# A windowed-attention and geglu block on one Trainium2 core: a third copy buffer, a band in bf16, weights loaded slice by slice, and a sixth group of down corrections by seven products

## The chip, the core and the metric

The kernel runs on one core of one Trainium2 chip. TensorE (PE) multiplies matrices, VectorE (DVE), ScalarE (ACT) and GpSimd (POOL) work on what it leaves, and SyncE (SP) and ScalarE issue the transfers. Each engine takes its instructions in one fixed order and waits by semaphores for the others. The metric is the device time in microseconds (us) of one execution.

## The reference, cut to what matters

S = 2048 tokens, D = 640, H = 32 heads of 20, a window of 256 keys, F = 1536.

```python
def _A_ref(x, wqkv, wo):                     # x is layer-normed
    q, k, v = split((x @ wqkv))              # 32 heads of 20
    scores = einsum("bhqd,bhkd->bhqk", q, k) * 20 ** -0.5
    mask = (i - j >= 0) & (i - j < 256)
    p = softmax(where(mask, scores, -1e9))
    return einsum("bhqk,bhkd->bhqd", p, v) @ wo
h  = x + _A_ref(_layernorm(x), wqkv, wo)
h2 = h + (gelu(_layernorm(h) @ w_gate) * (_layernorm(h) @ w_up)) @ w_down
```

## The kernel before, in words

Everything is float32, and the big products are made on TensorE from 16-bit parts: a matrix is scaled by a power of two and split into a high half and a low half, and a product is three products of halves (high x high, high x low, low x high). For a part of the feed-forward matrices a scheme with sums replaces the plain one and saves a product in eight ("seven products").

**Stages.** (1) Load and split the three attention weights and the first tokens; (2) for chunks of 256 tokens, make queries and keys (the matmuls `mm<-xh,w0h` and the like for queries, `mm<-xh,w1h` for keys), copy them as two halves (`qks`), send them to DRAM (`qk`) and stack them into `qT` and `kT`; (3) for every block of 128 tokens compute scores by way of the wide banks `ra` and `rb`, first for the maxima (DVE's custom operation `junk<-ra` and `junk<-rb`, which also adds a mask or the `band`), then for the exponentials `pt` (ACT), mask them (POOL), multiply by the values (`pv<-pt,v`) and by the output weight; (4) the feed-forward, in 12 groups: 4 chunks of 512 tokens by 3 parts of F, each of 4 tiles of gate and up (`tp`, `ra`, `rb`) and then the down product (`mm`, `pv`).

**Who sets the order.** Every instruction goes through one helper, so the profile gives all of them line 199, and groups are told apart by tile names. A planner in `block_kernel` keeps a clock of estimated times for each engine while it writes the program. Each strand of work (a "lane": `load_lane`, `scale_lane`, `split_lane`, `qk_out`, `token_sums`, `dense_lane` and so on) says what its next step needs, and the loop at the end issues the first lane whose step could start about now. So a change of one buffer or one wait moves instructions on every engine. Until the first block has been scored, the loop issues a filler product where nothing else could run on TensorE:

```python
        else:
            if not pos["score"] and nc.t["tensor"] <= now:
                nc.tensor.matmul(pv[:, 0, :], ident16, ident16, start=True, stop=True)
```

In the trace they are `pv<-ident`; 235 of them run.

**Copies of queries and keys.** `qk_out` (L761): ACT writes the high half of one or two 128-column tiles into a `qks` buffer, DVE subtracts and writes the low half, ACT issues the transfer. There are two buffers, so the third copy waits until the first has been sent, and the `mm` bank that it reads stays full that long.

**Band.** `max_out` (L916) reads `band`, a 128x320 constant, beside the scores in PSUM, 448 times.

**Weights of the feed-forward.** The first gate, up and output weights come by slices (`wsl`). The other seven, `rest` in `load_lane` (L1641), are the down weight of part 0 and then gate, up and down of parts 1 and 2. Each is loaded whole into one staging tile `wst`, after the one before it is wholly split (`rest[i - 1].ready`). `scale` takes the largest absolute value of each slice, `split` writes the high half (ACT), and `low` the low half (DVE or POOL). A down weight is [128, 4, 640]: four slices of 640.

**Seven products.** `ORDER` lists the 12 groups, (0,0), (1,0), (0,1), (0,2), (1,1), (1,2) and then chunk 2 and chunk 3. For the groups in `SEVEN = ORDER[FIRST7:-1]`, with `FIRST7 = 6` five of them, the down product is `down7` (L1461): 88 matmuls of 320 columns, where `down` takes 96. It wants, for each such group, sums of the down weight (`seven_weights`: `ts`, two instructions of POOL and two of DVE, 1280 columns each) and of the tokens' factors (`seven_tokens`: `w9l`, four of POOL and four of DVE, 512 columns each). Eight results a group go by way of ACT into `w8l` and are added by DVE (`ht<-ht,w8l`, eight of 320 columns), and two come from the bank `pv`. `ah` and `al` are the halves of gelu(gate) times up, `gel` and `rs` its steps; `w10`, `w11`, `w12` are the halves of the down weights of parts 0, 1 and 2; `h0h`, `h0l`, `h1h`, `h1l` the normed tokens; `ws` the sums of gate and up weights.

Of the kernel before, what the change touches and what calls it, by code (L numbers as in the profile page):

```python
# [11 lines left out]
F32 = mybir.dt.float32  # L12
# [241 lines left out]
def block_kernel(ctx: ExitStack, tc: tile.TileContext, x, wqkv, wo, wg, wu, wd, out):  # L254
# [69 lines left out]
    def on(eng, *reads, when=None, after=None):  # L324
        f = need(*reads, when=when, eng=eng)
        if after is not None:
            return (eng,), lambda: max(f(), nc.others(after, eng))
        return (eng,), f
# [14 lines left out]
    nc.vector.tensor_copy(ident16, ident)  # L343
    mhalf = const.tile([P, 1], F32, name="mhalf")
    nc.vector.memset(mhalf, -0.5)
    ones = const.tile([P, P], F32, name="ones")
    nc.vector.memset(ones, 1.0)


    NS = 16  # L350
# [3 lines left out]
    class Weight:  # L354
# [5 lines left out]

        def __init__(self, src, shape, col, e=WE):
            self.src, self.shape, self.col, self.e = src, shape, col, e
            self.have = set()
            self.raw = {}

        @property
        def ready(self):
            return len(self.have) == self.shape[0]

        def load(self, room):  # L370
            for i in range(self.shape[0]):
# [16 lines left out]
            pos["used"] += self.sliced  # L388

        def scale(self, lane, tp="tp"):  # L390
            n = self.shape[0]
            am = nc.tile(lnp, [P, 8], F32, "am" + lane, 2 if lane == "0" else 1)
            nc.vector.memset(am[:, n:n + 1], _pow2(-100))
            for i in range(n):
                if self.hl and self.col != C_K:

                    yield on("scalar", self.raw[0, i])
                    nc.scalar.activation(self.hl[0][:, i, :], self.raw[0, i], AF.Abs,
                                         accum_out=am[:, i:i + 1])
                    continue  # L400
                yield on("vector", when=lambda: (0, i) in self.raw)
                yield on("vector", self.raw[0, i])
                nc.vector.tensor_reduce(am[:, i:i + 1], self.raw[0, i], axis=AX.X, op=ALU.max,
                                        apply_absolute_value=True)
                self.done_with()
            yield on("vector", am)
            nc.vector.tensor_reduce(am[:, 7:8], am[:, 0:n + 1], axis=AX.X, op=ALU.max)

            yield on("vector", am)
            nc.vector.tensor_scalar(am[:, 7:8], am[:, 7:8], _pow2(-self.e), None, op0=ALU.mult)  # L410
            hold = SETTLE if ffpools[1] else 0.0
            bound = need(am, slots=[tp])
            yield ("tensor",), lambda: bound() + hold
            t = bank(tp)
            nc.tensor.matmul(t[:, 0:P], am[:, 7:8].to_broadcast([P, P]), ident, start=True,
                             stop=True)
            pc = pw[:, self.col:self.col + 1]
            sc = sw[:, self.col:self.col + 1]
            yield soon("vector", t)
            nc.vector.tensor_reduce(am[:, 6:7], t[:, 0:P], axis=AX.X, op=ALU.max)  # L420
            done(tp)
            yield on("vector", am)
            nc.vector.tensor_scalar(pc.bitcast(I32), am[:, 6:7].bitcast(I32), 0x7F800000, None,
                                    op0=ALU.bitwise_and)
            yield on("vector", pc)
            nc.vector.tensor_scalar(sc.bitcast(I32), pc.bitcast(I32), -1, 0x7F000000,
                                    op0=ALU.mult, op1=ALU.add)
            self.scaled = True
            yield on("vector", pc)
            nc.vector.tensor_scalar(pc, pc, _pow2(self.e), None, op0=ALU.mult)  # L430
            self.known = True
# [6 lines left out]
        def split(self, pool, spread=0):  # L438
            self.room(pool)
            self.begun = True  # L440
            sc = sw[:, self.col:self.col + 1]
            for i in range(self.shape[0]):
                yield on("scalar", when=lambda: (1, i) in self.raw)
                yield on("scalar", sc, self.raw[1, i])
                nc.scalar.activation(self.hl[0][:, i, :], self.raw[1, i], AF.Copy, scale=sc)
                tasks.append(self.low(i, sc, i < spread))

        def low(self, i, sc, spread):
            hi, lo = (t[:, i, :] for t in self.hl)
            w = self.raw[1, i]  # L450
            if spread:
                yield on("scalar", w)
                nc.scalar.activation(w, w, AF.Copy, scale=sc)
                yield on("gpsimd", w)
                nc.gpsimd.tensor_tensor(lo, w, hi, op=ALU.subtract)
            else:
                yield on("vector", hi)
                nc.vector.scalar_tensor_tensor(lo, w, sc, hi, op0=ALU.mult, op1=ALU.subtract)
            self.have.add(i)
            self.done_with()  # L460
# [129 lines left out]
    def ff_scales_down(fg):  # L590
# [23 lines left out]
    nc.gpsimd.memset(mask, 0.0)  # L614
    nc.gpsimd.affine_select(mask[:, P:2 * P], mask[:, P:2 * P], pattern=[[-1, P]],
                            compare_op=ALU.is_ge, fill=NEG, base=0, channel_multiplier=1)
    band = wp.tile([P, 5 * HB], F32, name="band")
    nc.gpsimd.memset(band, 0.0)
    for a in range(2):
        first, last = band[HB * a:HB * a + HB, 0:HB], band[HB * a:HB * a + HB, 4 * HB:]  # L620
# [143 lines left out]
    def qk_out(c, which, ts, ps, d, left):  # L764

        o = ps[:, :len(ts) * CW].rearrange("p (t n) -> p t n", n=CW)
        up = qs if c == which == 0 else _pow2(QE)
        yield on("scalar", ps, when=lambda: pos["qk"] < pos["qks"] + 2 and (c or pos["qs"]))
        pos["qk"] += 1
        st = nc.tile(wq, [P, 2, 2, CW], F16, "qks", 2)  # L770
        hi, lo = (st[:, :len(ts), i, :] for i in range(2))
        nc.scalar.activation(hi, o, AF.Copy, scale=up)
        yield on("vector", hi, after=ps)
        nc.vector.scalar_tensor_tensor(lo, o, up, hi, op0=ALU.mult, op1=ALU.subtract)
        done("mm")
        both = st[:, :len(ts)].rearrange("p t m n -> p t (m n)")
        yield on("scalar", both)
        nc.scalar.dma_start(d[ts[0] * P:(ts[-1] + 1) * P].rearrange("(t p) m n -> p t (m n)", p=P),
                            both)
        pos["qks"] += 1  # L780
        left[0] -= 1
        if not left[0]:
            for blocks in [[2 * c, 2 * c + 1]] if c < 2 else [[2 * c], [2 * c + 1]]:
                side.append((LATE, stack(c, which, d, blocks)))
# [346 lines left out]
    NCH = S // (CB * P)  # L1131
    ORDER = [(0, 0), (1, 0), (0, 1), (0, 2), (1, 1), (1, 2)]
    ORDER += [(c, fg) for c in range(2, NCH) for fg in range(FG)]
    PLAIN, FIRST7 = 3, 6
    hts, ga = {}, {}
    ffpools = [None, None]

# [434 lines left out]
        if chunk[c] == CB:  # L1572
            side.append((LATE, token_sums(c)))

    TS, sums = {}, {}

    def token_sums(c):
        hh, hl = hT[c]
        h1, h2 = hh[:, :, :CW], hh[:, :, CW:]
        l1, l2 = hl[:, :, :CW], hl[:, :, CW:]  # L1580
        yield on("vector", when=lambda: ffpools[1] and (c < 2 or W["d", FG - 1].ready))
        t = (nc.tile(ffp, [P, KC, 512], F32, "ts" if c else "ts0") if c % 2 or not c else
             nc.tile(ffpools[0], [P, KC, 512], F32, "wst")).bitcast(F16)
        t = t.rearrange("p c (a n) -> p a c n", a=4)
        for ks in (slice(k, k + 1) for k in range(KC)):
            a, b, m, d = (t[:, i, ks] for i in range(4))
            yield on("vector", h1, h2)
            nc.vector.tensor_tensor(a, h2[:, ks], h1[:, ks], op=ALU.subtract)
            yield on("vector", a, l2)
            nc.vector.scalar_tensor_tensor(b, a, -_pow2(-TE), l2[:, ks], op0=ALU.mult, op1=ALU.add)  # L1590
            yield on("vector", b, l1)
            nc.vector.tensor_tensor(d, l1[:, ks], b, op=ALU.subtract)
            yield on("vector", l2, h2)
            nc.vector.scalar_tensor_tensor(m, l2[:, ks], _pow2(TE), h2[:, ks], op0=ALU.mult,
                                           op1=ALU.subtract)
        TS[c] = t
# [44 lines left out]
    def load_lane():  # L1641
        for w in weights[NW:NW + 3]:
            for turn in range(2):
                yield from w.load_slices(turn)
        rest = weights[NW + 3:]
        for i, w in enumerate(rest):
            yield ("sync",), need(when=lambda: ffpools[0] and (i < 1 or rest[i - 1].ready),
                                  eng="sync")
            t = nc.tile(ffpools[0], [P] + w.shape, F32, "wst")
            w.load([t[:, k, :] for k in range(w.shape[0])])  # L1650

    def scale_lane(todo, lane):
        for i in todo:
            w = weights[i]
            before = {2: W["k"]}.get(i)
            yield on("vector", when=lambda: (w.loaded or w.sliced) and (not before or before.scaled)
                     and (i < NW or B[0].maxima == H) and (i <= NW or B[0].scored))
            yield from w.scale(lane, "ra" if i < NW else "tp")
            if i == 0:
# [313 lines left out]
```

## Time and profile before

| | before |
|---|---|
| time, median of 3 runs | 999.64 us (998.12 to 999.91) |
| the profiled execution | 998.68 us; its span in the trace 997.0 us |
| mean granted clock of TensorE | 0.998 |
| TensorE busy | 976.7 us (98%) |
| VectorE busy | 790.4 us (79%) |
| ScalarE busy | 485.7 us (49%) |
| GpSimd busy | 341.6 us (34%) |

A matmul's row shows its own length, which is longer than its turn: successive 320-column rows overlap, so a product's price is read from the distance between two starts. Idle time stands in square brackets behind a row, with the instruction that ended it. A transfer row of a queue (SPq, ACTq) is the time of its issue. Windows rows give, for a stretch, the busy time of PE, of its weight loads, DVE, ACT and POOL, then TensorE's granted clock (1.00 is 2.4 GHz, 0.50 is 1.2 GHz), the share of DMA time and GB/s.

### The profile page before, as it was taken

Reading aid. Unit: us, or ns where it says so; the run is one execution under the profiler, and the core shown is the slowest. Engines: PE = TensorE matmul, PEld = TensorE weight load, DVE = VectorE, ACT = ScalarE, POOL = GpSimd, SP = SyncE. Lnnn points to the kernel's source line nnn. Section 1 sums busy time; section 2 is a strip of 40 time slices with the busy share of each in tenths; the row PEclk is TensorE's granted clock in tenths of the full one; section 3 lists DMA queues with packets and bytes.
Section 4 is the critical chain, followed back from the end, with each engine's and each line's share of the span. In section 5 each row is a group of like instructions: output and inputs, shape, how many; then the busy total and the mean of one; then the engine's idle time right before and its main releaser. Section 6 shows DMA issues by size and latency. Waiting matters only on the chain.

```text
span 997.0 us, 35791 instructions
## 1 busy us (share of the span) xinstructions
PE 976.7 (98%) x15326; PEld 746.1 (75%) x15326; DVE 790.4 (79%) x2246; ACT 485.7 (49%) x859; POOL 341.6 (34%) x498
## 2 busy tenths in 40 slices
PE   8998999999999999999999999999999999999998
PEld 7875777777877777777755754688788888888886
DVE  7878998887866776776797796888976887788784
ACT  5515647575555555555576634343223333443431
POOL 7003335464433333333344411253403223233320
PEclk9999999999999999999999999999999999999999
DMA  8658666743622432222304441234353442223211
GB/s 314 141 112 175 154 166 173 169 128 82 128 72 68 97 93 74 76 73 63 134 16 118 98 154 57 98 135 132 116 184 106 146 146 80 80 80 107 81 54 53
DMA packets 129616, 113.01 MB, mean 113 GB/s; under 512 B 85169, under 2 KB 103345, under 8 KB 129457
## 3 DMA queue, kind: packets, MB, share of 16 engines
q1 hardware_dynamic: 117360, 99.97, 35.8%
q10 hardware_dynamic: 12096, 10.75, 3.4%
q8 instruction: 120, 1.97, 0.8%
q14 instruction: 40, 0.32, 0.1%
HBM read 73.73 MB, written 28.84 MB: 103 GB/s over the span
## 4 chain that ended last, share of the span: by engine, by line
PE 83%; DVE 9%; ACT 3%; DMA 2%; issue 1%; POOL 1%; SPq 0%; ACTq 0%; DVEq 0%
PE mm L199 40%; PE ra L199 12%; PE rb L199 12%; PE pv L199 11%; PE tp L199 9%; DVE junk L199 2%; DVE ht L199 1%; ACT pt L199 1%; DVE wsl L199 1%; DMA qT<-mT 1%; DVE gel L199 1%; DMA qT<-in_wqkv_dram 1%; DVE w1l L199 0%; DMA wst<-in_wu_dram 0%; ACT wst L199 0%
## 5 line engine op out<-in xcount | busy, mean ns | idle before, releaser
L199 POOL TENSOR_SCALAR_AFFINE_SELECT pt<-pt 128x512 f32<-128x512 f32 x352 | 175.4, 514 | 276.9 <-ACT pt L199 259.5
L199 DVE CUSTOM_DVE_ANT_0 junk<-rb,band 128x320 bf16<-128x320 f32 x232 | 113.3, 488 | 36.4 <-PE rb L199 31.2
L199 ACT ACTIVATE pt<-ra,esc 128x640 f32<-128x640 f32 (+2 forms) x132 | 100.4, 768 | 83.1 <-PE ra L199 70.6
L199 ACT ACTIVATE pt<-rb,esc 128x640 f32<-128x640 f32 (+2 forms) x124 | 94.1, 766 | 80.5 <-PE rb L199 78.0
L199 DVE CUSTOM_DVE_ANT_0 junk<-ra,band 128x320 bf16<-128x320 f32 x216 | 105.6, 489 | 34.3 <-PE ra L199 29.3
L199 PE MATMUL pv<-pt,v 128*21 128x128 f32 x2880 | 102.9, 275 | 0.3 <-ACT oT L199 0.2
L199 PEld LDWEIGHTS <-ws 128*128 128x128 f16 x720 | 70.7, 98 | 13.5 <-issue 3.2
L199 PEld LDWEIGHTS <-ah 128*128 128x128 f16 x648 | 63.4, 98 | 23.0 <-issue 0.6
L199 PEld LDWEIGHTS <-qT 60*64 60x64 f16 x1280 | 29.7, 104 | 62.6 <-issue 50.7
L199 PEld LDWEIGHTS pv<-pt,v 128*21 128x21 f32 x2880 | 69.0, 100 | 9.8 <-issue 1.1
L199 PEld LDWEIGHTS <-kT 62*64 62x64 f16 x2880 | 64.4, 106 | 10.8 <-issue 5.9
L199 PEld LDWEIGHTS <-gu 128*128 128x128 f16 (+1 forms) x697 | 51.5, 98 | 25.5
L199 DVE SCALAR_TENSOR_TENSOR ht<-mm,ffk,ht 128x320 f32<-128x320 f32 x86 | 46.9, 545 | 14.3 <-PE mm L199 13.0
L199 PE MATMUL mm<-xh,w1h 128*32 128x256 f16 (+1 forms) x344 | 55.9, 273 | 1.2 <-DVE qks L199 1.2
L199 ACT CAST ah<-gel 128x512 f16<-128x512 f32 x48 | 29.6, 617 | 54.4 <-DVE gel L199 52.8
L199 PE MATMUL mm<-xl,w1h 128*32 128x256 f16 (+1 forms) x362 | 56.0, 273 | 0.0
L199 PE MATMUL mm<-xh,w1l 128*32 128x256 f16 (+1 forms) x356 | 55.9, 273 | 0.0
L199 DVE TENSOR_TENSOR al<-gel,ah 128x512 f16<-128x512 f32 x48 | 43.3, 903 | 12.8 <-ACT ah L199 11.9
L199 PE MATMUL mm<-w3h,oh 128*32 128x320 f16 (+1 forms) x373 | 49.7, 299 | 0.6 <-DVE ht L199 0.6
L199 PE MATMUL mm<-w3h,ol 128*32 128x320 f16 (+1 forms) x361 | 49.7, 299 | 0.0
L199 PE MATMUL mm<-w3l,oh 128*32 128x320 f16 (+1 forms) x364 | 49.7, 299 | 0.0
L199 PE MATMUL mm<-xh,w0l 128*32 128x256 f16 (+1 forms) x361 | 49.3, 273 | 0.0
(354 smaller groups left out, 2645.7 us busy)
## 6 DMA issues: line engine op xcount, KB each, us to landing
ws<-wsums SPq DMA_DIRECT2D x24, 640.0 KB
qk<-qks ACTq DMA_DIRECT2D x32, 256.0 KB
wsums<-ws SPq DMA_DIRECT2D x12, 640.0 KB
qT<-qk SPq DMA_DIRECT2D x72, 80.0 KB
kT<-qk SPq DMA_DIRECT2D x72, 80.0 KB
ht<-in_x_dram SPq DMA_DIRECT2D x16, 320.0 KB
h_dram<-ht SPq DMA_DIRECT2D x16, 320.0 KB
ht<-h_dram SPq DMA_DIRECT2D x16, 320.0 KB
```

The lines of the kernel that those rows point to most:

```text
L199: r = real(*args, **kw)
```

## The change

Five edits. (a) A constant `ones`, which nothing reads, goes. (b) `band` is bf16 instead of float32. (c) `qks` has three buffers. (d) The seven later weights go through one tile `stages[0]`, slice by slice: slice i of a weight is loaded as soon as slice i of the weight before it is split. Down weights are taken as five slices of 512 columns, and the largest values are taken as slices arrive. (e) `FIRST7` is 5, so that group (1,2) too goes by `down7`.

```diff
-    ones = const.tile([P, P], F32, name="ones")
-    nc.vector.memset(ones, 1.0)
...
             self.src, self.shape, self.col, self.e = src, shape, col, e
+            self.n = shape[0]
...
-            return len(self.have) == self.shape[0]
+            return len(self.have) == self.n
+
+        def load_pieces(self, room, prev):
+            self.n = KC
+            src = self.src.rearrange("p a b -> p (a b)")
+            for i in range(KC):
+                yield ("sync",), need(when=lambda: not prev or i in prev.have, eng="sync")
+                self.raw[0, i] = self.raw[1, i] = room[:, i, :]
+                nc.sync.dma_start(room[:, i, :], src[:, i * 512:(i + 1) * 512])
+            self.loaded = True
...
-    band = wp.tile([P, 5 * HB], F32, name="band")
+    band = wp.tile([P, 5 * HB], BF16, name="band")
...
-        yield on("scalar", ps, when=lambda: pos["qk"] < pos["qks"] + 2 and (c or pos["qs"]))
+        yield on("scalar", ps, when=lambda: pos["qk"] < pos["qks"] + 3 and (c or pos["qs"]))
         pos["qk"] += 1
-        st = nc.tile(wq, [P, 2, 2, CW], F16, "qks", 2)
+        st = nc.tile(wq, [P, 2, 2, CW], F16, "qks", 3)
...
-    PLAIN, FIRST7 = 3, 6
+    PLAIN, FIRST7 = 3, 5
...
-        for i, w in enumerate(rest):
-            yield ("sync",), need(when=lambda: ffpools[0] and (i < 1 or rest[i - 1].ready),
-                                  eng="sync")
-            t = nc.tile(ffpools[0], [P] + w.shape, F32, "wst")
-            w.load([t[:, k, :] for k in range(w.shape[0])])
+        yield ("sync",), need(when=lambda: ffpools[0], eng="sync")
+        stages.append(nc.tile(ffpools[0], [P, KC, 512], F32, "wst"))
+        for prev, w in zip([None] + rest, rest):
+            yield from w.load_pieces(stages[0], prev)
```

**TensorE in the ramp, before the first maxima.** Here `gu`, `h0h`, `h0l` are the value weight's slices, w1 is the key weight and w0 the query weight. Before, all the key products have been issued, the value products of the first block stop half way, and fillers begin:

```order
L199 MATMUL mm<-xl,w1h 128x256
L199 LDWEIGHTS w1l
L199 MATMUL mm<-xh,w1l 128x256
L199 MATMUL rb<-ident,pt 128x128 x4
L199 MATMUL tp<-ident,pt 128x128
L199 MATMUL mm<-h0h,gu 128x320
L199 MATMUL mm<-h0l,gu 128x320 x2
L199 LDWEIGHTS ident_81
L199 MATMUL pv<-ident_81 128x128
```

And of the changed kernel:

```order
L199 MATMUL mm<-h0l,gu 128x320
L199 MATMUL mm<-gu 128x320
L199 MATMUL mm<-h0h,gu 128x320 x2
L199 MATMUL mm<-h0l,gu 128x320 x2
L199 LDWEIGHTS w0h
L199 MATMUL mm<-xh,w0h 128x256
L199 LDWEIGHTS w0h
L199 MATMUL mm<-xl,w0h 128x256
L199 LDWEIGHTS w0l
L199 MATMUL mm<-xh,w0l 128x256
```

The last two rows of the first piece repeat 86 times before the value products go on. In the second both halves of the first block's value products run through, and the query products of the next chunk follow at once. Further on there, 34 key products of a third chunk stand ahead of the first maxima too, and the second block's value products after them; a run of 30 fillers between the maxima and the first scores is down to 12, with one of 19 ahead of it. All in all 144 fillers are left of 235.

**GpSimd before the third chunk's first group.** `w9l` are the token sums of a group with seven products, `ws<-gu` sums of gate and up weights, `lyh` and `lyi` steps of two tokens' norms. Before:

```order
L199 TENSOR_TENSOR lyh<-lveh,mhalf 128x1
L199 TENSOR_TENSOR lyi<-lvei,mhalf 128x1
L199 TENSOR_TENSOR ws<-gu 128x640
L199 TENSOR_TENSOR ws<-gu,ws 128x640
L199 TENSOR_TENSOR w9l<-w9l,ah 128x512
L199 TENSOR_TENSOR w9l<-ah 128x512
```

And of the changed kernel:

```order
L199 TENSOR_TENSOR w9l<-w9l,ah 128x512
L199 TENSOR_TENSOR ws<-gu,ws 128x640
L199 TENSOR_TENSOR w9l<-ah 128x512
L199 TENSOR_TENSOR lyh<-lveh,mhalf 128x1
L199 TENSOR_TENSOR ws<-gu 128x640
L199 TENSOR_TENSOR w9l<-w9l,ah 128x512
L199 TENSOR_TENSOR ws<-gu,ws 128x640
L199 TENSOR_TENSOR w9l<-ah 128x512
L199 TENSOR_TENSOR lyi<-lvei,mhalf 128x1
```

The new token sums stand among the weight sums and the norms instead of behind them.

**VectorE in the same place.** `wsl` are rows of tokens being normed. Before:

```order
L199 TENSOR_SCALAR wsl<-wsl,lmvi,lyi 128x640
L199 SCALAR_TENSOR_TENSOR ht<-mm,ffk,ht 128x320
L199 TENSOR_TENSOR rs<-ra,gelt 128x256
L199 SCALAR_TENSOR_TENSOR gel<-rs,ffk,gel 128x512
L199 TENSOR_TENSOR wsl<-wsl 128x640
L199 TENSOR_TENSOR al<-gel,ah 128x512
```

And of the changed kernel, for the other of the two norms:

```order
L199 TENSOR_SCALAR wsl<-wsl,lmvh,lyh 128x640
L199 SCALAR_TENSOR_TENSOR w9l<-w9l,al 128x512
L199 TENSOR_TENSOR rs<-ra,gelt 128x256
L199 TENSOR_TENSOR ht<-ht,w8l 128x320
L199 SCALAR_TENSOR_TENSOR gel<-rs,ffk,gel 128x512
L199 TENSOR_TENSOR wsl<-wsl 128x640
L199 SCALAR_TENSOR_TENSOR ht<-pv,ffk,ht 128x320
L199 SCALAR_TENSOR_TENSOR ht<-mm,ffk,ht 128x320
L199 TENSOR_TENSOR al<-gel,ah 128x512
```

Between the same steps of a norm and of gelu there are now a token sum (`w9l`) and the additions from `w8l` and `pv`, ahead of the `gel`, `ht` and `rs` instructions that free TensorE's banks.

## Rows read from the trace of the kernel before

**Rows 1.** The page: busy time, share of the span, instructions.
```profile
PE 976.7 (98%) x15326; PEld 746.1 (75%) x15326; DVE 790.4 (79%) x2246; ACT 485.7 (49%) x859; POOL 341.6 (34%) x498
```

**Rows 2.** Waits of TensorE: line waited for, us in total, times, longest.
```profile
PE pv L199 <- DVE pv L199: 2.5, 1, 2.5
PE tp L199 <- ACT rr L199: 2.2, 1, 2.2
...
PE ra L199 <- DVE mxs L199: 1.9, 1, 1.9
```

**Rows 3.** Chain of waits, 30 to 84 us: start, us, what.
```profile
37.79 4.80 PE pv L199 x86
...
53.23 0.24 PE ra L199 x8
```

**Rows 4.** Timeline of TensorE, 70 to 79 us: start, us, instruction.
```profile
71.34 0.27 PE L199 MATMUL mm<-xh,w1l 128*128 128x256 f16 x1
71.45 1.84 PE L199 MATMUL pv<-ident 128*128 128x128 f16 x30
73.13 0.30 PE L199 MATMUL mm<-w2h,xh 128*128 128x320 f16 x1
```

**Rows 5.** Timelines of ACT, DVE and SP's queue, 34 to 46 us.
```profile
35.05 0.38 ACT L199 ACTIVATE qks<-mm 128x256 f16<-128x256 f32 x1 [1.05 <-DMA qk<-qks]
39.66 0.34 ACTq L199 DMA_DIRECT2D qk<-qks  x1
...
39.89 5.94 SPq L199 DMA_DIRECT2D kT<-qk  x6
```

**Rows 6.** Timeline of VectorE, 52 to 55 us: the first maximum.
```profile
53.52 0.29 DVE L199 CUSTOM_DVE_ANT_0 junk<-ra,mask 128x128 bf16<-128x128 f32 x1 [2.00 <-PE ra L199]
```

**Rows 7.** Timeline of VectorE, 71 to 77 us.
```profile
76.07 0.42 DVE L199 CUSTOM_DVE_ANT_0 junk<-rb,mask 128x256 bf16<-128x256 f32 x1
...
76.42 0.42 DVE L199 SCALAR_TENSOR_TENSOR qks<-mm,qks 128x256 f16<-128x256 f32 x1
```

**Rows 8.** Timeline of TensorE, 706 to 713 us.
```profile
706.60 0.30 PE L199 MATMUL mm<-w12l,ah 128*128 128x320 f16 x1
706.74 0.30 PE L199 MATMUL mm<-w12h,al 128*128 128x320 f16 x1
709.23 0.99 PE L199 MATMUL tp<-h1l,ws 128*128 128x256 f16 x5 [2.19 <-ACT rr L199]
```

**Rows 9.** Busy times by stretch.
```profile
68.00:155.00 87.00, 82.85 (x1532) 60.48 (x1529) 79.32 (x293) 47.42 (x87) 29.09 (x42) 1.00 0.69 159
709.60:712.80 3.20, 3.20 (x18) 2.21 (x16) 3.20 (x5) 0.99 (x2) 0.00 (x0) 0.50 0.41 100
767.00:822.00 55.00, 55.00 (x471) 45.85 (x470) 45.37 (x100) 18.96 (x42) 14.19 (x10) 1.00 0.51 160
820.00:856.00 36.00, 36.00 (x311) 30.16 (x309) 29.24 (x45) 14.49 (x33) 10.50 (x7) 1.00 0.22 75
```

**Rows 10.** VectorE's groups, 820 to 892 us: two groups with seven products.
```profile
L199 DVE TENSOR_TENSOR ht<-ht,w8l 128x320 f32<-128x320 f32 x16 | 13.2, 842 | 1.4 <-ACT w8l L199 1.4
L199 DVE TENSOR_TENSOR al<-gel,ah 128x512 f16<-128x512 f32 x8 | 9.7, 1210 | 2.7 <-ACT ah L199 2.4
L199 DVE SCALAR_TENSOR_TENSOR w9l<-w9l,al 128x512 f16<-128x512 f16 x4 | 5.3, 1328 | 1.4 <-POOL w9l L199 1.4
L199 DVE SCALAR_TENSOR_TENSOR w9l<-al,ah 128x512 f16<-128x512 f16 x4 | 2.7, 682 | 0.0
L199 DVE SCALAR_TENSOR_TENSOR ts<-ts,w11h 128x1280 f16<-128x1280 f16 x1 | 1.5, 1481 | 0.0
```

**Rows 11.** Timeline of VectorE, 703 to 856 us.
```profile
705.25 2.85 DVE L199 TENSOR_SCALAR wsl<-wsl,lmvi,lyi 128x640 f32<-128x640 f32 x1
...
837.44 2.12 DVE L199 TENSOR_TENSOR ht<-ht,w8l 128x320 f32<-128x320 f32 x1
...
847.30 0.48 DVE L199 TENSOR_TENSOR ht<-ht,w8l 128x320 f32<-128x320 f32 x1
...
850.30 0.69 DVE L199 TENSOR_TENSOR al<-gel,ah 128x512 f16<-128x512 f32 x1
```

**Rows 12.** Timeline of GpSimd, 702 to 837 us.
```profile
705.16 2.60 POOL L199 TENSOR_TENSOR ts<-w10l 128x1280 f16<-128x1280 f16 x1
...
806.71 1.16 POOL L199 TENSOR_TENSOR w9l<-ah 128x512 f16<-128x512 f16 x1
...
836.60 2.61 POOL L199 TENSOR_TENSOR ts<-ts,w11l 128x1280 f16<-128x1280 f16 x1 [3.93 <-PE pv L199]
```

More of the change, by code (lines that the diff above doesn't have):

```diff
@@ L367, in ready, with parts @@
         def ready(self):
-            return len(self.have) == self.shape[0]
+            return len(self.have) == self.n
[7 more added lines that the diff above has]
+            self.loaded = True
+        def parts(self, i):
+            if self.n == self.shape[0]:
+                return [t[:, i, :] for t in self.hl]
+            return [t.rearrange("p a b -> p (a b)")[:, i * 512:(i + 1) * 512] for t in self.hl]
         def load(self, room):
@@ L390, in scale @@
         def scale(self, lane, tp="tp"):
-            n = self.shape[0]
+            n = self.n
             am = nc.tile(lnp, [P, 8], F32, "am" + lane, 2 if lane == "0" else 1)
@@ L441, in split @@
             sc = sw[:, self.col:self.col + 1]
-            for i in range(self.shape[0]):
+            for i in range(self.n):
                 yield on("scalar", when=lambda: (1, i) in self.raw)
                 yield on("scalar", sc, self.raw[1, i])
-                nc.scalar.activation(self.hl[0][:, i, :], self.raw[1, i], AF.Copy, scale=sc)
+                nc.scalar.activation(self.parts(i)[0], self.raw[1, i], AF.Copy, scale=sc)
                 tasks.append(self.low(i, sc, i < spread))
         def low(self, i, sc, spread):
-            hi, lo = (t[:, i, :] for t in self.hl)
+            hi, lo = self.parts(i)
             w = self.raw[1, i]
@@ L1573, in norm_lane @@
             side.append((LATE, token_sums(c)))
-    TS, sums = {}, {}
+    TS, sums, stages = {}, {}, []
     def token_sums(c):
@@ L1582, in token_sums @@
         t = (nc.tile(ffp, [P, KC, 512], F32, "ts" if c else "ts0") if c % 2 or not c else
-             nc.tile(ffpools[0], [P, KC, 512], F32, "wst")).bitcast(F16)
+             stages[0]).bitcast(F16)
         t = t.rearrange("p c (a n) -> p a c n", a=4)
@@ L1655, in scale_lane @@
             before = {2: W["k"]}.get(i)
-            yield on("vector", when=lambda: (w.loaded or w.sliced) and (not before or before.scaled)
+            yield on("vector", when=lambda: (w.loaded or w.sliced or (0, 0) in w.raw) and (not before or before.scaled)
                      and (i < NW or B[0].maxima == H) and (i <= NW or B[0].scored))
```

## Prediction

> **What bounds the kernel now.** I read the busy times first: TensorE is busy 98% of the span, VectorE 79%, the others half or less [rows 1]. So whatever takes work off TensorE pays in full as long as nobody else becomes late, and whatever takes time off another engine pays only where TensorE waits for it. The waits of TensorE come next: the longest single ones are 2.5, 2.2 and 1.9 us, and each happens once [rows 2]. There is little idle time to win. What the busy time hides is work that computes nothing: the fillers. In the chain of waits a run of 86 stands from 37.79 us for 4.80 us [rows 3], and the timeline has a run of 30 at 71.45 us that takes 1.84 us [rows 4]. They are counted as busy, so the reader has to look for them by name.
>
> Then the stretches. From 68 to 155 us VectorE works 79.32 of 87 us, 91%, while TensorE has 82.85: attention starts close to VectorE's limit. From 767 to 822 us, ahead of the third chunk's groups, TensorE is busy 55.00 of 55 and VectorE 45.37. From 820 to 856 us, a whole group with seven products, TensorE has 36.00 of 36 and VectorE 29.24 [rows 9].
>
> **The change part by part.** All sums are against the profiled execution, 998.68 us (its span is 997.0, and 1.7 us lie around it). The median shown is 999.64, 0.96 higher; I add that at the end, and it is no more than the spread of the three runs.
>
> *Fillers (third buffer).* Before, ACT makes the last copy of the first key products at 35.05 us, after 1.05 us of waiting for the transfer of an earlier buffer; its own transfer goes out at 39.66 and the stack into kT at 39.89 [rows 5]. Meanwhile the planner had nothing for TensorE, hence the 86 fillers. With a third buffer it finds query products to issue there, and then 34 key products more ahead of the first maxima. 235 fillers become 144. At 4.80/86 = 55.8 ns each [rows 3], 91 fewer are 5.08 us. The work that takes their place was due later anyway, so the whole is a gain if TensorE isn't made to wait instead. Does the new order wait? Walking it with the trace's distances, the added dense work ends and the first maxima start at about 52.7 us, 0.5 earlier than the 53.23 of the chain [rows 3]. The kT stack, issued from 39.89 for 5.94 us [rows 5], is through long before, and VectorE stood idle 2.00 us ahead of its first maximum [rows 6]. On the way I find two short waits of about 0.2 us. I take a gain of 5.1 and a loss of 0.4. Bounds: nothing gained, if each filler becomes idle time, and 5.1.
>
> *Seven products for group (1,2).* 96 matmuls become 88, so eight go. Two starts in a row lie 706.74 - 706.60 = 0.14 us apart [rows 8]: 8 x 0.14 = 1.1 us off TensorE. The price lies on the other engines. VectorE gets eight additions `ht<-ht,w8l`, undisturbed 0.48 us [rows 11], four token sums of 0.68 and two weight sums of 1.48 [rows 10]: 3.84 + 2.72 + 2.96 = 9.5 us. GpSimd gets four token sums of 1.16 and two weight sums of 2.60 [rows 12], 9.8 us. All of it falls into what is 767 to 822 us before. There VectorE has 45.37 of 55 [rows 9]; with 9.5 it has 54.9, and TensorE's work there shrinks to 53.9. And VectorE slows down beside GpSimd: in two groups with seven products 16 additions took 842 ns instead of 480, eight `al` 1210 instead of 690 (the undisturbed row at 850.30), four `w9l` 1328 instead of 682 [rows 10, 11]. That is 5.8 + 4.2 + 2.6 = 12.6 us, 6.3 a group. Should all of this come on top, VectorE needs 61.2 us where TensorE needs 53.9, 7.3 too much.
>
> The Trainium skill, SBUF — State Buffer, section Who interferes with whom, says why: a VectorE instruction with both inputs in SBUF shares a read port with GpSimd and is blocked wholly, not slowed, for as long as the other's instruction holds it. The rows agree: the addition of 2.12 us at 837.44 ends 0.35 us after GpSimd's weight sum (836.60, 2.61 us), and the norm's scaling that took 2.85 us at 705.25 began 0.09 us after one of 2.60 [rows 11, 12]. By the rule alone the ceiling would be GpSimd's whole added 9.8 us instead of 6.3, and VectorE 10.8 us over.
>
> So the bounds of this price are 0 and 7.3 us of waiting. For 0 speaks that a whole group with the same VectorE work and the same disturbance leaves TensorE 36.00 of 36 busy, with VectorE at 29.24 [rows 9]. But there no weight sums and no norms of the next chunk are due, and here the new GpSimd work stands among them, as the order shows. I take 2 us: the nearest row says 0, the sum says 7.3, and the buffers of TensorE's results and the easier quads in the middle of the stretch absorb some.
>
> *Band in bf16.* It is read beside PSUM by all maxima with three key blocks. Before shows none with a 16-bit second operand, but a subtraction of 256 columns from PSUM with an f16 second operand takes 0.42 us, just as a maximum of 256 columns with a float32 mask does [rows 7]. So I take 0. Bounds: a few per cent of these maxima either way; in the stretch where VectorE is near its limit, 68 to 155 us, up to 1 us.
>
> *Weights slice by slice.* The same bytes by 15 transfers of 512 columns instead of 12 of 640 for the down weights, three transfers, three reductions and three splits more, all behind hundreds of microseconds of TensorE at 98%. What it moves is when ACT and VectorE split, and SP's queue: each slice's load waits there for a split, and behind it wait the reloads of token rows and the weight sums. They are wanted no earlier than the third chunk, after 790 us. I take 0; if that cover is gone, a late `wsl` stops TensorE like the 2.2 us for `rr` [rows 2], so the bounds are 0 and 2 us.
>
> *Reshuffled order elsewhere.* Between 68 and 155 us VectorE sets the pace and the instructions stand in other places: TensorE's idle time there, 87 - 82.85 = 4.15 us [rows 9], may go by half or grow by half, so -2 to +2, and I take 0. The wait of 2.19 us at 709.23 stays: ACT's `rr` stood behind a cast that waited for the slow `wsl` of 705.25 [rows 8, 11], and neither that stretch's instructions nor their order on VectorE change. After it 3.20 us ran at granted clock 0.50, which is 1.2 GHz, and half of them, 1.6 us, is lost work [rows 9]; that stays with it. `ones` goes at nothing: its memset is at the start, on an engine nobody waits for then.
>
> Sum: -5.1 + 0.4 - 1.1 + 2.0 = -3.8, so 994.9 on the profiled execution's scale and about 995.5 to 996 on the median's. I say 995.2, between the two scales.
>
> **Rivals.**
> 1. *VectorE stops TensorE in the sixth group* (the slower side). Place: what is 767 to 822 us before. 7.3 us of waiting, in pieces over 2 us, each followed by a stretch at half clock like that at 709.6, 1.6 us a piece; with two, 10.5. 998.68 - 5.8 + 10.5 = 1003.4, on the median's scale about 1004 (5.8 is what the ramp and the eight products give). It decides from about 6 us of waits on: below it the ramp still pays. For it: the sum of 61.2 against 53.9. Against: VectorE's instructions there are placed by the planner with their own times counted, only the disturbance isn't.
> 2. *The fillers turn into waits.* The first maxima hang on kT and on VectorE, and up to 155 us VectorE at 91% [rows 9] sets attention's pace. Then dense work done ahead is missing there as fill, and TensorE idles. Gain 1.1, minus 0.4 to 2 elsewhere: about 999. Against it: idle time before the first maximum on VectorE, and dense work of later chunks that the planner can pull in.
> 3. *More goes than the fillers.* The reshuffled attention loses half its idle time (-2), the sixth group costs nothing, and the wait at 709 with its half clock goes (2.2 + 1.6): 998.68 - 5.8 - 2 - 3.8 = 987; with one or two of the three, about 990.
> 4. *A queue holds back.* SP's slice loads delay the token reloads, one or two waits of 2 us with half clock: 994.9 + 4 = 999.
>
> **How the numbers follow.** Forecast 0.55, rival 1 0.14, rival 2 0.12, rival 3 0.14, rival 4 0.05. A measurement of this kernel can tell about 0.2%, 2 us, from no change. Faster by more than that, under 997.6: nearly all of the forecast (0.53) and rival 3 (0.14), and the mild end of rivals 2 and 1 (0.05), 0.72. Slower, over 1001.6: two thirds of rival 1 and a little of 2, 0.10. Within: the rest, 0.18. The range takes rival 3 to 989.5 and goes up through rivals 2 and 4 into rival 1, to 1001. The forecast's own range is 992.5 to 998.
>
> **What would show it.** Right: no `pv<-ident` run between 35 and 53 us, and the first maxima near 52.7; between 750 and 830 us VectorE busy over 92%, and TensorE's waits there for `ht`, `gel` or `rs` adding up to 1 to 4 us; the 2.2 us for `rr` still there with its half clock; `junk<-rb,band` still near 488 ns. Wrong: idle TensorE between 35 and 100 us grown by several us (rival 2), a granted clock of 0.50 between 750 and 830 us (rival 1), waits for `wsl` or `wst` transfers (rival 4), or `band` maxima under 450 ns.

## The result, and the profile after

The changed kernel takes 1003.19 us (median of 17 runs, 999.66 to 1006.02), the kernel before 999.42 (17 runs): ratio 1.0040, 95% interval 1.0028 to 1.0052. It is slower, where I forecast 995.2 and a range up to 1001.

The profiled execution of the changed kernel is one of the quick ones, 1001.18 us with a span of 999.5. Its busy times:

```profile
PE 972.1 (97%) x15467; PEld 742.9 (74%) x15467; DVE 804.3 (80%) x2265; ACT 489.1 (49%) x870; POOL 349.1 (35%) x504
```

TensorE has 4.6 us less to do than in [rows 1] and the span is 2.5 us longer: 7 us more of waiting. The waits of TensorE (line waited for, us in total, times, longest):

```profile
PE tp L199 <- ACT rr L199: 5.9, 2, 3.7
PE pv L199 <- DVE pv L199: 2.4, 1, 2.4
PE ra L199 <- DVE rs L199: 2.2, 2, 1.6
```

In [rows 2] there is one wait for `rr`, of 2.2 us. Now there are two, one of 3.7 us, and waits for VectorE's `rs`, which before has none of. Busy times by stretch, in the columns of [rows 9]; the last row is the stretch right after the new wait:

```profile
68.00:155.00 87.00, 84.23 (x1703) 62.12 (x1705) 79.16 (x293) 48.15 (x88) 27.59 (x42) 1.00 0.61 152
...
767.00:822.00 55.00, 49.09 (x404) 40.13 (x403) 52.26 (x97) 20.17 (x44) 21.84 (x15) 0.97 0.42 138
830.00:866.00 36.00, 36.00 (x310) 30.13 (x308) 29.92 (x48) 15.00 (x34) 10.33 (x6) 1.00 0.21 74
```

```profile
784.25:787.40 3.15, 3.15 (x15) 2.23 (x15) 3.15 (x7) 0.84 (x2) 0.00 (x0) 0.50 0.70 208
```

From 767 to 822 us TensorE falls from 55.00 to 49.09 us, VectorE rises from 45.37 to 52.26, 95% of the stretch, and GpSimd from 14.19 to 21.84 [rows 9]. After the wait TensorE runs 3.15 us at granted clock 0.50, 1.2 GHz, which loses 1.6 us more. A whole later group with seven products (830 to 866) is as before.

Where the wait comes from, seen in four timelines (start, us, instruction, idle time before). TensorE:

```profile
779.87 0.71 PE L199 MATMUL mm<-w12h,ah 128*128 128x320 f16 x4
784.25 1.23 PE L199 MATMUL tp<-h0l,ws 128*128 128x256 f16 x5 [3.67 <-ACT rr L199]
```

ScalarE, where `rr` stands behind the cast of a normed row, and the cast behind VectorE:

```profile
783.20 0.72 ACT L199 CAST wsl<-wsl 128x640 f16<-128x640 f32 x1 [4.96 <-DVE wsl L199]
783.83 0.37 ACT L199 COPY rr<-tp 128x256 f32<-128x256 f32 x1
```

VectorE, three instructions that took 1.64, 1.88 and 3.10 us where [rows 10] has 0.682 for the second, and the same `gel` takes 0.74 at 784.42:

```profile
771.84 1.64 DVE L199 SCALAR_TENSOR_TENSOR gel<-rs,ffk,gel 128x512 f32<-128x512 f32 x1
...
774.26 1.88 DVE L199 SCALAR_TENSOR_TENSOR w9l<-al,ah 128x512 f16<-128x512 f16 x1
...
784.42 0.74 DVE L199 SCALAR_TENSOR_TENSOR gel<-rs,ffk,gel 128x512 f32<-128x512 f32 x1
...
794.25 3.10 DVE L199 SCALAR_TENSOR_TENSOR gel<-rs,ffk,gel 128x512 f32<-128x512 f32 x1
```

And GpSimd, whose instructions end at 772.94, 775.59 and 796.80, each 0.54 or 0.55 us before VectorE's stretched instruction does:

```profile
771.34 1.60 POOL L199 TENSOR_TENSOR w9l<-ah 128x512 f16<-128x512 f16 x1
...
774.14 1.45 POOL L199 TENSOR_TENSOR ws<-gu 128x640 f16<-128x640 f16 x1
...
794.19 2.61 POOL L199 TENSOR_TENSOR ts<-w10l 128x1280 f16<-128x1280 f16 x1 [5.75 <-PE mm L199]
```

Against the typical time of each instruction, VectorE loses 10.6 us in this way between 767 and 823 us, and 3.6 before in the same place (11.1 and 3.0 if the typical time is the median in the same trace).

The ramp's products went as written: in the chain of waits, where 86 fillers stood [rows 3], there are products.

```profile
37.76 6.52 PE mm L199 x42
```

The score products for the first maxima start at 52.83 us, where I had about 52.7. But only one of them runs; the next waits 0.93 us for a transfer into `kT`, and VectorE's first maximum comes at 54.34 us, 0.8 later than before [rows 6] (TensorE, VectorE, then SP's queue):

```profile
52.83 0.24 PE L199 MATMUL ra<-kT,qT 60*64 60x128 f16 x1
53.99 0.30 PE L199 MATMUL ra<-kT,qT 60*64 60x128 f16 x7 [0.93 <-DMA kT<-qk]
```

```profile
54.34 0.29 DVE L199 CUSTOM_DVE_ANT_0 junk<-ra,mask 128x128 bf16<-128x128 f32 x1 [3.94 <-PE ra L199]
```

```profile
41.40 9.33 SPq L199 DMA_DIRECT2D kT<-qk  x6
```

The stack into `kT` is issued from 41.40 for 9.33 us, where before it went from 39.89 for 5.94 [rows 5]. The last value product comes at 557.87 us after 559.28, 1.4 us earlier: TensorE's busy time up to there fell by 3.75 us (546.29 to 542.54), and its idle time rose by 2.3. These are single executions. Experiments 1, 5, 6 and 11 have TensorE's order of the changed kernel up to there, and their last value products come at 557.98, 562.13, 558.66 and 559.28 us.

### The profile page after: what moved, and what is told of

It reads as the page before. It is cut to its first block, busy times and chain, and to the rows that moved or that the text cites. A ratio compares the mean times of both kernels' runs of the same rounds, so it can differ in the third digit from the quotient of the medians.

```text
span 999.5 us, 36110 instructions
## 1 busy us (share of the span) xinstructions
PE 972.1 (97%) x15467; PEld 742.9 (74%) x15467; DVE 804.3 (80%) x2265; ACT 489.1 (49%) x870; POOL 349.1 (35%) x504
## 4 chain that ended last, share of the span: by engine, by line
PE 80%; DVE 11%; DMA 3%; ACT 2%; issue 2%; POOL 1%; SPq 0%; ACTq 0%; DVEq 0%
PE mm L199 39%; PE rb L199 11%; PE ra L199 11%; PE pv L199 10%; PE tp L199 9%; DVE junk L199 2%; DVE ht L199 1%; DVE gel L199 1%; ACT pt L199 1%; POOL pt L199 1%; DVE ts L199 1%; DMA qk<-qks 1%; DMA wsl<-in_wu_dram 1%; DVE w1l L199 1%; DVE w9l L199 0%
## 5 line engine op out<-in xcount | busy, mean ns | idle before, releaser
L199 ACT ACTIVATE pt<-ra,esc 128x640 f32<-128x640 f32 (+2 forms) x128 | 97.6, 768 | 85.2 <-PE ra L199 78.3
L199 DVE CUSTOM_DVE_ANT_0 junk<-ra,band 128x320 bf16<-128x320 f32 x222 | 108.5, 489 | 37.3 <-PE ra L199 32.2
L199 DVE CUSTOM_DVE_ANT_0 junk<-rb,band 128x320 bf16<-128x320 f32 x226 | 110.5, 489 | 32.8 <-PE rb L199 28.1
L199 ACT ACTIVATE pt<-rb,esc 128x640 f32<-128x640 f32 (+2 forms) x128 | 96.9, 765 | 80.5 <-PE rb L199 64.3
L199 PEld LDWEIGHTS <-ah 128*128 128x128 f16 (+1 forms) x648 | 61.2, 98 | 22.6 <-issue 1.0
L199 ACT ACTIVATE gel<-gel,ffk 128x512 f32<-128x512 f32 x36 | 26.0, 722 | 54.2 <-DVE gel L199 54.2
```

The lines of the kernel that those rows point to most:

```text
L199: r = real(*args, **kw)
```

## The experiments

Each is quoted as expected before it ran; S, R, C, D and P are the theories named there. Numbers follow the labels; 3 (the kernel before with the third buffer, the bf16 band and no constant) has no result. Ratios are to the kernel before, run beside it, with their 95% intervals.

**1. Five groups again.**

```diff
-    PLAIN, FIRST7 = 3, 5
+    PLAIN, FIRST7 = 3, 6
```

> The changed kernel with FIRST7 back at 6, so that group (1,2) goes by 96 plain matmuls again; all else as changed. Theory S (the sixth group stops TensorE between 767 and 830 us): the profile of the changed kernel shows waits of 3.67, 1.6 and 0.6 us there and about 1.6 us of lost work at half clock, some 7.5 us, for 1.1 us of matmuls saved. Taken back, they go: 1003.2 - 7.5 + 1.1 = about 997 to 998, ratio to the kernel before 0.997 to 0.999. Rival R (the new order up to the end of attention costs it): no more than 1 us moves, about 1002 to 1003.

Measured 998.43, ratio 0.9976 (0.9962 to 0.9989). Between 767 and 822 us TensorE works all the time again:

```profile
767.00:822.00 55.00, 55.00 (x471) 45.83 (x470) 44.34 (x97) 18.90 (x42) 12.23 (x10) 1.00 0.48 143
```

The sixth group costs 1.0040 - 0.9976 = 0.0064, 6.4 us. R is out.

**2. Six groups on the kernel before.**

```diff
-    PLAIN, FIRST7 = 3, 6
+    PLAIN, FIRST7 = 3, 5
```

> The kernel before with FIRST7 = 5 and nothing else. Theory S: 999.4 + 5 to 6 = 1004.5 to 1005.5, with a wait of TensorE over 2 us for ACT's rr between 770 and 790 us and VectorE busy over 92% from 770 to 830. Rival R: 998.3, the 1.1 us of eight matmuls less.

Measured 1007.59, ratio 1.0071 (1.0056 to 1.0085). The waits of TensorE from 760 to 840 us are those of the changed kernel:

```profile
PE tp L199 <- ACT rr L199: 3.7, 1, 3.7
PE ra L199 <- DVE rs L199: 2.2, 2, 1.9
```

The one edit, by itself, costs 7.1 us, and the time is 2 to 3 us more than theory S gave. Its profiled execution also fell to half clock near 98 us, where the profiled execution before did not (granted clock 0.98 from 68 to 155 us), in the part where the two programs are the same.

**4. The cast later in ScalarE's queue.**

```diff
-        yield on("scalar", src, when=lambda: not opened[key] and (not when or when()))
+        f = need(src, when=lambda: not opened[key] and (not when or when()), eng="scalar")
+        yield ("scalar",), lambda: f() + (0.0 if dst else 2.0)
```

> The changed kernel with one edit: in the norms of the feed-forward's tokens ACT's cast of wsl is put into the program only when its source has been ready for 2 us by the planner's clock, so that a late wsl doesn't hold back the copy rr behind it. Six groups stay. Theory S in its narrow form (the wait is ACT's queue: rr behind the cast): the waits of 3.67 us at 780 and of 2.2 us at 704 and the half clock go, 1003.2 - 5 to 7 = 996 to 998.5. In its broad form (VectorE itself is too slow there, and any order waits): the waits move to gel, rs or ht, about 1001 to 1003. Rival R: 1003.

Measured 1002.32, ratio 1.0022 (1.0012 to 1.0032): the broad form. The wait for `rr` is gone from 760 to 840 us, and the waits for VectorE's `rs` have grown from 2.2 to 3.8 us:

```profile
PE ra L199 <- DVE rs L199: 3.8, 3, 2.5
```

So ScalarE's queue only passes on that VectorE is late: with the cast out of the way, TensorE waits for VectorE itself.

**5. Plain copies on ScalarE for the sixth group's token sums.**

```diff
-                nc.gpsimd.tensor_tensor(s2, s1, h1, op=ALU.subtract)
+                nc.scalar.copy(s2, s1)        # group (1,2) only
...
-                nc.gpsimd.tensor_tensor(s3, h1, h2, op=ALU.subtract)
+                nc.scalar.copy(s3, h1)        # group (1,2) only
```

> The changed kernel with six groups, where for group (1,2) alone GpSimd's four token sums w9l are left out and ACT writes four plain copies in their place (so this group's down corrections are not the reference's). VectorE's added work stays whole. Theory C (it is GpSimd beside VectorE, whose two-input instructions stop while GpSimd reads): the waits between 765 and 790 us go, of about 7.5 us some 4 to 5; 1003.2 - 4.5 = about 998.5 to 999. Theory D (VectorE's added 9.5 us alone is too much): no more than 1 us moves, about 1002 to 1003.

Measured 1005.94, ratio 1.0061 (1.0047 to 1.0076): neither. TensorE waits for ScalarE, whose cast waits for a transfer that still reads its buffer (TensorE, then ScalarE):

```profile
797.45 1.22 PE L199 MATMUL pv<-ts,w9l 128*128 128x320 f16 x4 [4.07 <-ACT w8l L199]
```

```profile
795.18 0.72 ACT L199 CAST wsl<-wsl 128x640 f16<-128x640 f32 x1 [4.19 <-DMA h1h<-wsl]
```

The edit brought a wait of its own. The 3.67 us for `rr` are gone in it, but `rr` stands ahead of the cast here, as in experiment 4, so it doesn't settle C or D. Experiment 11 asks again without ScalarE.

**6. Eight additions left out.**

```diff
-            nc.vector.tensor_tensor(o, o, z, op=ALU.add)
+            if g:
+                nc.vector.tensor_tensor(o, o, z, op=ALU.add)
```

> The changed kernel with six groups, where for group (1,2) alone VectorE's eight additions ht<-ht,w8l are left out (so those results lack them): 8 x 0.48 = 3.84 us less on VectorE undisturbed, GpSimd as it was. Theory D: waits fall by about 4 us, 999. Theory C: the sums on GpSimd still stop VectorE in the same instructions, the long waits stay to more than half, 1000.5 to 1002.

Measured 998.79, ratio 0.9990 (0.9977 to 1.0003), as D had it. 3.84 us less of plain VectorE work bring 5 us. TensorE, 767 to 822 us, is at 52.28 instead of 49.09, at full clock:

```profile
767.00:822.00 55.00, 52.28 (x443) 43.06 (x442) 52.22 (x98) 20.49 (x46) 24.90 (x16) 1.00 0.45 140
```

So VectorE's load holds TensorE up there, and 2.7 us of waiting are left. It doesn't tell whether its own work or the disturbance took it over.

**7. Five groups and the late cast.** The edits of 1 and 4 together.

> Five groups, as in the first experiment, and the late cast of the fourth. There the cast took the 2.2 us for rr near 704 us away. If the rest of the kernel is as in the first (998.4): 996 to 996.5, better than both. If the cast's other order costs in attention, as the last value product at 560.56 instead of 557.87 in the fourth suggests: 998.5 to 999.

Measured 996.23, ratio 0.9971 (0.9959 to 0.9982), within the interval of experiment 1: the late cast's worth isn't shown by it.

**8. Two buffers for the copies.**

```diff
-        yield on("scalar", ps, when=lambda: pos["qk"] < pos["qks"] + 3 and (c or pos["qs"]))
+        yield on("scalar", ps, when=lambda: pos["qk"] < pos["qks"] + 2 and (c or pos["qs"]))
-        st = nc.tile(wq, [P, 2, 2, CW], F16, "qks", 3)
+        st = nc.tile(wq, [P, 2, 2, CW], F16, "qks", 2)
```

> Five groups as in the first experiment, and qks back at two buffers; the band in bf16 and the slices stay. What the third buffer alone is worth. My prediction's step: 4.7, so 998.4 + 4.7 = 1003. By the trace of the changed kernel (fillers of 5.1 us became 3.3 us of other waits): 998.4 + 1.3 to 2 = 1000. Should the gain of the first experiment come from the slices: 998.4.

Measured 1007.78, ratio 1.0074 (1.0046 to 1.0102): 9 to 10 us over experiment 1, outside all three expectations, and worse than the kernel before, which has two buffers too. Its six executions lie far apart: the profiled one kept granted clock 1.000 and took 1000.36 us, the others, at 0.992 to 0.995, took 1006.29 to 1011.42. What is left of the change in this kernel is the band, the slices and the missing constant. The band alone leaves every order up to the feed-forward as it was; the missing constant does not, so it was tried by itself.

**9. The kernel before without the constant.**

```diff
-    ones = const.tile([P, P], F32, name="ones")
-    nc.vector.memset(ones, 1.0)
```

> The kernel before without the unused constant and its memset, nothing else. My prediction priced this edit at nothing. The memset counted 0.2 us on the planner's clock for VectorE, so the program's order changes from the first microseconds on, and 262 fillers are written instead of 235. If the order before 560 us is a matter of such small shifts (theory P): 3 to 7 us slower, as the eighth experiment's two buffers, whose order is the same up to the scores of about the second half of attention: 1003 to 1007. If the edit is worth nothing: 1000.

Measured 1007.96, ratio 1.0074 (1.0049 to 1.0099). A dead memset taken out makes the kernel 7 us slower. From 68 to 155 us, against 82.85 us at full clock in [rows 9]:

```profile
68.00:155.00 87.00, 79.84 (x1387) 56.73 (x1386) 75.90 (x285) 45.52 (x83) 26.54 (x38) 0.94 0.70 154
```

TensorE is busy 3 us less there, and 6% of its clock, at most some 5 us, is lost as well. Up to the ramp the programs are the same but for that memset and a few fillers; from about 28 us on the planner, whose VectorE clock is 0.2 us behind, writes another order. Experiment 8 has this order up to about 480 us and costs the same in the median. Its execution at 1000.36 us shows that the order need not cost 7 us: over the same TensorE instructions up to 480 us, experiment 9's execution falls some 5 us behind it, partly in longer waits for transfers into `kT` and `qT`, partly where the clock is halved.

**10. The constant kept, all else as in experiment 1.**

```diff
+    ones = const.tile([P, P], BF16, name="ones")
+    nc.vector.memset(ones, 1.0)
```

> Five groups, third buffer, bf16 band and slices as in the first experiment, and the constant with its memset put back (in bf16, where it fits). 140 fillers. This is the third buffer, band and slices against the kernel before without the constant's shift of the order. My prediction's step: 4.7 less than before, 995.5. Theory P (the constant's shift and the buffer's shift are both changes of the planner's order, and each can fall either way): anything from 996 to 1003, and no sum of single effects.

Measured 994.75, ratio 0.9951 (0.9933 to 0.9969). With the constant that the kernel before has, buffer, band and slices are worth 4.9 us (3.1 to 6.7): the 4.7 of my prediction.

**11. All sums of the seven products on VectorE, six groups.**

```diff
-            nc.gpsimd.tensor_tensor(t1, d2, d1, op=ALU.subtract)
+            nc.vector.tensor_tensor(t1, d2, d1, op=ALU.subtract)
...
-                nc.gpsimd.tensor_tensor(s2, s1, h1, op=ALU.subtract)
+                nc.vector.tensor_tensor(s2, s1, h1, op=ALU.subtract)
```

(and t3 and s3 likewise, with what they wait on).

> The changed kernel with six groups, where the sums for the seven products that GpSimd makes (token sums w9l, weight sums ts) are made by VectorE, in all six groups; the output is the reference's. VectorE gets four instructions of 512 columns and two of 1280 more a group, by its 256-column row (0.28 us) about 4 x 0.5 + 2 x 1.2 = 4.4 us; GpSimd leaves it alone there. Theory C (disturbance; 10.6 us of VectorE's time between 767 and 823 us in the changed kernel): net 3 to 6 us less on VectorE, the waits fall by about as much, 998 to 1000. Theory D (VectorE's own load): 4 us more on it, 1005 to 1007.

Measured 993.46, ratio 0.9942 (0.9921 to 0.9963): theory C, and more. VectorE has 94% of the stretch, nearly as in the changed kernel, with four more instructions in the sixth group's tokens alone, and TensorE hardly waits:

```profile
767.00:822.00 55.00, 54.93 (x469) 45.68 (x467) 51.83 (x116) 23.59 (x51) 6.84 (x5) 1.00 0.45 146
```

TensorE's 15467 matmuls stand in the same order in both traces. Between 700 and 840 us the changed kernel's TensorE waits 8.1 us (5.9 for `rr`, 2.2 for `rs`) and loses 1.6 at half clock, 9.7 in all; here it waits for nothing between 700 and 840 us that the profile lists, and the ratios are 0.0098 apart. About 7.5 of it belong to the sixth group, the rest to the older wait for `rr` near 707 us. `rr` stands ahead of the cast here too, but experiment 4 has shown that this alone only moves the wait. And none of the waits is for `w9l` or `ts` themselves, so it isn't that the sums come sooner.

The groups of VectorE from 815 to 890 us (busy, mean ns) show why the move is so cheap:

```profile
L199 DVE TENSOR_TENSOR ht<-ht,w8l 128x320 f32<-128x320 f32 x17 | 8.1, 482 | 0.7 <-ACT w8l L199 0.7
L199 DVE TENSOR_TENSOR al<-gel,ah 128x512 f16<-128x512 f32 x9 | 6.1, 683 | 0.0
...
L199 DVE TENSOR_TENSOR w9l<-ah 128x512 f16<-128x512 f16 x4 | 1.7, 422 | 0.0
...
L199 DVE TENSOR_TENSOR ts<-w11l 128x1280 f16<-128x1280 f16 x1 | 0.8, 816 | 0.0
```

The additions are back from 842 to 482 ns and `al` from 1210 to 683 [rows 10], and the sums take 0.42 and 0.82 us, where GpSimd took 1.16 and 2.60 [rows 12].

**12. Whole weights.**

```diff
-                yield ("sync",), need(when=lambda: not prev or i in prev.have, eng="sync")
+                yield ("sync",), need(when=lambda: not prev or prev.ready, eng="sync")
```

> Five groups, third buffer, bf16 band as in the first experiment, but each later weight's slices wait until the weight before is wholly split, as before the change. All engines' orders stay the same up to about 510 us. The prediction's step (slices: 0 to 2 us): 998.4 within 1 us. If slices are worth something in the late attention: over 1 us away.

Measured 998.87, ratio 0.9985 (0.9971 to 1.0000), as experiment 1 within the intervals: starting a slice's load before the whole weight is split is worth nothing that can be measured. (The cut into slices of 512 columns stays in this run.)

**13. Constant kept, six groups, sums on VectorE.** The edits of 10 (without its five groups) and 11.

> The changed kernel with six groups, the constant and its memset kept (as in the tenth experiment) and all sums of the seven products on VectorE (as in the eleventh). If the two repairs add: 1003.2 x (0.9951/0.9976) x (0.9942/1.004) of the ratios, that is a ratio of about 0.992, 991 to 992. If the order's shift takes it back: 0.994 to 0.996.

Measured 989.38, ratio 0.9895 (0.9878 to 0.9912), the best of all and 10 us better than the kernel before. Against experiment 11, the constant alone is worth 0.0047, and the intervals don't meet. The two repairs add, and a little more comes than the 0.992 of their product.

**14. The same with five groups.** The edits of 13 and 1.

> The same with five groups. With GpSimd's disturbance gone, does the sixth group pay its 1.1 us? If VectorE then has room: 0.5 to 1.5 us slower than the thirteenth. If VectorE's added 9.5 us still stop TensorE: the same or faster.

Measured 991.08, ratio 0.9909 (0.9891 to 0.9927). 1.4 us slower than 13 in the median, but the intervals overlap, and the medians differ by how many executions kept the clock: at granted clock 1.000, five of experiment 13's six took 988.67 to 989.42 us and three of these six took 989.22 to 989.57. In 13's profile TensorE still waits 1.5 us for ScalarE's `rs` near the sixth group, about what the eight matmuls save. So that the sixth group pays now is not shown. That it no longer costs 6 us is shown.

**15. Experiment 13 and the late cast.**

> The thirteenth with the late cast of the fourth. In the eleventh's profile no wait for rr is left between 700 and 830 us, so the late cast has nothing to win there: within 1 us of the thirteenth, or up to 2 us slower by its other order in attention.

Measured 992.94, ratio 0.9925 (0.9911 to 0.9939): 3 us slower than 13 in the median, where 2 was the most expected. The programs are the same up to about 530 us, and this profiled execution is 2.4 us behind 13's at 256 us already, after a wait of 2.5 us for `kT` (0.9 in 13) with half clock behind it; the one execution at 1.000 took 990.67. So little of the 3 us is shown to be the cast's. What speaks against its place as the cause is experiment 4.

## Why the prediction was wrong, point by point

*Fillers: right in size, wrong on `kT`, and half lost in this order.* 5.1 gained and 0.4 lost was the step. The fillers went, and the score products began at 52.83 us as worked out. That the stack into `kT` is through long before was wrong: TensorE waits 0.93 us for it, and VectorE's first maximum is 0.8 us later than before instead of earlier. With the constant kept the gain is there (experiment 10, 4.9 us, slices and band in it, which are worth nothing; in experiment 13 the last value product comes at 553.99 us, 5.3 earlier than before). In the changed kernel only about half of it arrives (experiment 1, 2.4 us).

*`ones` at nothing: the first step that failed.* "Its memset is at the start, on an engine nobody waits for then" is beside the point. The program's order hangs on the planner's clock, and 0.2 us there gave another ramp. The price is 7.4 us on the kernel before (9), 4.7 with all else repaired (13 against 11) and, less surely, 2.5 in experiment 10 against 1, where the intervals overlap. Part of the 7.4 is half clock, and how much of that comes differs from execution to execution (8). I had compared the orders of the changed kernel with those of before as a whole, and put all of the difference down to the buffer.

*Sixth group: the step that failed most.* I took 2 us between 0 and 7.3 and "the nearest row says 0". Measured: 6.4 and 7.1 us with the eight matmuls' 1.1 already in it, so 7.5 to 8.2. The trace has it as 5.9 us of waits and 1.6 of half clock. The upper bound of 7.3 us of waiting, worked out from the rows of the disturbance, was much nearer than 2, and rival 1 had its place, its wait, and the half clock after it. That rival 1's 1003.4 lies so close to the measured 1003.2 is luck: it had 10.5 us where 7.5 came, and 4.7 from the ramp where 2.4 came. The row that I went by was from a stretch where the weight sums and the norms of the next chunk are absent; I had named that difference and then not let it count. Experiment 11 shows the cause: without GpSimd's sums TensorE doesn't wait, though VectorE is nearly as busy and TensorE's order is the same. The rule of the Trainium skill (SBUF — State Buffer, Who interferes with whom), that a two-input VectorE instruction stops for as long as GpSimd holds the shared port, agrees with the 3.10 us of 794.25 beside 2.61 us; it spoke against the change, and I should have given it more weight. The ceiling that I drew from it, 10.8 us over, was more than the 5.9 us of waits that came.

*Why some 95% of VectorE's time is enough in one kernel and not in the other:* my reading, not tried by itself, is that the planner counts undisturbed times. In the eleventh experiment they hold, and every result that frees a bank is due when planned; in the changed kernel 10.6 us come unplanned, ahead of `gel` and `rs`.

*Band:* its maxima take 489 ns, as before: right. *Slices:* 0, right (12). *The wait at 709:* still there, 2.2 us (at 707 us in the changed kernel), but its half clock, which I said stays with it, does not: the granted clock of the profiled execution is 1.00 from 700 to 740 us. The wait was put down to GpSimd's weight sum beside the norm's scaling, and it goes with the sums (11).

*Sum:* with what was measured for the parts, -4.9 (buffer, band, slices), +2.5 (order) and +6.4 (sixth group with its matmuls) are +4.0, and the changed kernel is 3.8 us slower. This is no proof of the parts: the three are the steps from the kernel before by experiments 10 and 1 to the changed kernel, and must add up to it.

## What to carry to other kernels

Where a planner writes the order from estimated times, no edit is free: price a removed dead instruction by the order that comes out, and test each edit of a bundle alone before giving its effect to the one with the reason. When an engine is to get work where another holds it up, as GpSimd does VectorE here, add the stretched durations of the trace to its load, not the short ones, and take the row of the stretch where the work will lie. Moving small elementwise work to a helper engine can cost the main engine more than doing it itself: here a token sum on GpSimd (1.60 us at 771.34) stretched one VectorE instruction by 0.90 us, from 0.74 to 1.64, where VectorE makes such a sum in 0.42 us. And before a small difference of medians is given to an edit, compare executions at the same granted clock (14, 15).

## What the runs showed that was not expected

- 16-bit subtractions from SBUF to SBUF are far quicker on VectorE than on GpSimd: 0.42 against 1.16 us at 512 columns, 0.82 against 2.60 at 1280, 2.8 and 3.2 times. The Trainium skill's GPSIMD Engine Reference, section 3.1 (Elementwise — side-by-side cycle accounting), gives about two for float32 and says to use VectorE for such work.
- The same wait can be followed by full or half clock in the same order of instructions. In two kernels with one order up to 700 us, TensorE waits 1.22 us for `oT`, and then goes on at 1.00 or at 0.50. Of the changed kernel, and of experiment 5 (timelines of TensorE, then both kernels' row of 84 to 94 us, the changed one first):

```profile
88.30 0.42 PE L199 MATMUL pv<-pt,v 128*21 128x128 f32 x8 [1.22 <-ACT oT L199]
```

```profile
88.98 0.63 PE L199 MATMUL pv<-pt,v 128*21 128x128 f32 x8 [1.22 <-ACT oT L199]
```

```profile
84.00:94.00 10.00, 8.43 (x194) 5.54 (x190) 9.05 (x39) 5.13 (x13) 3.68 (x6) 1.00 0.36 117
```

```profile
84.00:94.00 10.00, 8.43 (x163) 5.17 (x161) 7.08 (x31) 4.16 (x10) 2.71 (x5) 0.83 0.43 135
```

  So a wait has its own length as its price and sometimes 1.6 us more. Much of the spread goes with it: the 17 runs of the changed kernel have mean granted clocks of 0.991 to 0.998, each 0.001 being about 1 us, while five of experiment 13's six runs have 1.000 and lie within 0.8 us.
